# Splitting the maxima's rows and multiplying the gates on GpSimd instead of VectorE, in a two-branch attention kernel

## The chip, the core and the metric

The kernel runs on one core of a Trainium2 chip. The core has five engines with a queue of instructions each, executed in order: TensorE (PE, its weight loads shown as PEld), VectorE (DVE), ScalarE (ACT), GpSimd (POOL) and SyncE (SP), which here only issues DMAs. An engine waits at an instruction until the semaphores of the work it needs have come. The metric is the device time of one execution in microseconds (us); lower is better.

## The reference

Two attention blocks over the same input are mixed by a gate per token. There are 2048 tokens of 512 features and 32 heads of 16.

```python
x = A_x
g = sigmoid((x * gate_w).sum(-1, keepdims=True))
# A: causal softmax inside 4 segments of 512 tokens, plus a memory of earlier segments
logits = einsum("bhqd,bhkd->bhqk", qs, ks) * scale + mask
a_dot  = softmax(logits) @ vs
a_mem  = (phi(qs) @ M) / (phi(qs) @ z + 1e-6)     # M, z summed over earlier segments
a = (sigmoid(beta) * a_mem + (1 - sigmoid(beta)) * a_dot) @ wo_A
# B: full softmax attention over 2048 tokens
b = (softmax(q @ k.T * scale) @ v) @ wo_B
out = g * a + (1 - g) * b
```

## The kernel before

A unit is four heads (a group `qd` of 8) and 512 queries (a segment `c`). Units 0 to 31 are A, units 32 to 63 are B. After a stage of projections (up to about 370 us) the main loop runs 32 rounds, k = 0 to 31. In round k TensorE computes the transposed scores of unit 32+k in 32 groups (`t_group`, L528), then those of unit k in 5 groups; ScalarE takes their exponentials (L534), GpSimd masks the diagonal pieces of A (L537), and TensorE multiplies with the values (`pv`, L550).

The softmax needs each query's maximum before the exponential. It is found one round ahead: TensorE also computes the scores of the next units the other way round (`s_b` L474, `s_a` L452) into two banks `sbk`, and VectorE reduces each bank to maxima (L476, L460, L462). `m_chain(k+1)` then turns the maxima of a pair of units (tile `mx`, 128 queries x 32) into two fp32 rows: `hi`, the negated maximum rounded to the matmul's format, and the rest, both in the tile `m8` (named `m` in the profile). `m_rows(k+1)` transposes `m8` on TensorE (L501), ScalarE copies it out (L503, tile `mr`), and SyncE's DMAs (L509) write it as extra rows of the query tiles `qa` and `qb`, so that the score product subtracts the maximum by itself.

A unit is finished by `fin_copy` (L557 and a DMA to `pd`), `fin_load` (loads the output `o` and the softmax sums `rec`), `fin_rec` (L574 to L580: the reciprocal of the sums, times the gate `grow`, and for A times `nq` from beta, then a DMA to `rd`), `fin_bc` (L586: `rd` broadcast into `d`) and `fin_norm` (L590 on GpSimd: `o` times `d`). `load_wo` (L601 to L603) loads a piece of the two output weights and splits it on GpSimd into `wh` and `wl`; it runs in rounds 1 to 4.

The order is written out by hand. A round has iterations `it`, two groups of TensorE each, and the function `beside` puts the smaller work at an iteration: `fin_rec` of the B unit at 5, its `fin_bc` and the `fin_rec` of the A unit at 6, `fin_norm` of B at 9 and of A at 13 (every other round), the loads of the next A queries, keys and values at 6, `load_wo` at 9, `m_chain` at 10. `m_rows` follows in TensorE's order behind group 24, the first of iteration 12. Each engine's own queue has its pieces in the order of this code:

```python
            beside(k, it)
            if it == S_LAST:
                m_chain(k + 1)
```

with `S_LAST = 10`, and further down in the same loop body, still ahead of the next iteration,

```python
            if it == 9:
                if k % 2 == 0 and k < 30:
                    load_vb(k // 2 + 1)
                if 1 <= k <= 4:
                    load_wo(k - 1)
```

Of the kernel before, what the change touches and what calls it, by code (L numbers as in the profile page):

```python
# [12 lines left out]
OP = mybir.AluOpType  # L13
# [21 lines left out]
def gated_mix_kernel(ctx, tc, xt, wq, wk, wv, wo, beta, wqkv, wob, gate_w, out):  # L35
    nc = tc.nc
# [18 lines left out]
    grow = P.tile([128, 2, NC4, E], FT, name="grow")  # L55
    gh = P.tile([128, 4], FT, name="gh")
    nh = P.tile([128, 4], FT, name="nh")
    nq = P.tile([128, 8], FT, name="nq")
# [374 lines left out]
    def pair_max(k):  # L433
        if k not in MX:
            MX[k] = W.tile([128, 2, 4, 4], FT, name="mx")
        return MX[k]
# [43 lines left out]
    def m_chain(k):  # L480
        mx = pair_max(k)
        if k == 1:
            nc.vector.memset(mx[:, 0], 0.0)
        if k < 32:
            nc.vector.tensor_reduce(mx[:, 1], MXB.pop(32 + k).rearrange("q j p i c -> q (j p) i c"), axis=AX.X,
                                    op=OP.max)
        else:
            nc.vector.memset(mx[:, 1], 0.0)
        del MX[k]
        mx = mx.rearrange("q u h i -> q (u h i)")  # L490
        m8 = M8[k] = W.tile([128, 2, 32], FT, name="m8")
        hi = W.tile([128, 32], FR, name="mhi")
        nc.vector.tensor_scalar(hi, mx, -1.0, None, op0=OP.mult)
        nc.vector.tensor_copy(m8[:, 0], hi)
        nc.vector.scalar_tensor_tensor(m8[:, 1], mx, -1.0, hi, op0=OP.mult, op1=OP.subtract)

    def m_rows(k):
        m8 = M8.pop(k)
# [72 lines left out]
    def fin_rec(u):  # L571
        kd, qd, c = UN[u]
        r = AT.pop(("r", u))
        nc.vector.reciprocal(r, r)  # L574
        if kd == "A":
            nc.vector.scalar_tensor_tensor(r, r, nq[:, qd:qd + 1], grow[:, 0, c], op0=OP.mult, op1=OP.mult)
        else:
            nc.vector.tensor_tensor(r, r, grow[:, 1, c], op=OP.mult)
        AT["rd", u] = D.tile([128, E], FT, name=f"rd{u}")
        nc.sync.dma_start(AT["rd", u], r)  # L580

# [168 lines left out]
    for blk in range(16):  # L750
        g, c = divmod(blk, 4)
# [37 lines left out]
        if blk == 14:  # L789
            m_chain(0)  # L790
# [96 lines left out]
    def beside(k, it):  # L887

        for f, it0, u in ((fin_load, NT + 1, 32 + k), (fin_rec, 5, 31 + k), (fin_bc, 6, 31 + k),
                          (fin_load, 1, k - 1), (fin_rec, 6, k - 1), (fin_bc, S_LAST + 2, k - 1)):  # L890
            if it == it0 and (k or it0 > NT):
                f(u)
        c, j = divmod(k - 1, 8)
        if k and j % 2:
            for kd, it0 in (("B", 9), ("A", 13)):
                if it == it0:
                    fin_norm(kd, j // 2, c)
        if k >= 8 and k % 2 == 0 and it == NT + 2:
            out_split(k // 8 - 1, k // 2 % 4)
        if (k, it) == (31, 4):  # L900
            grest = AT["grest"] = AT["o"][0][64:, 0, 0]
            nc.sync.dma_start(grest, GD[3 * C:].rearrange("(o t) -> o t", o=1).to_broadcast([64, C]))
        if (k, it) == (31, 9):
            grest = AT["grest"]
            nc.vector.tensor_scalar(grest, grest, nh[64:, 3:4], None, op0=OP.mult)
        if (k, it) == (31, NT + 2):
            fin_rec(63)
        if k == 31 and it == 13:
            o = AT["o"][1][:64, 3, 0]
            nc.gpsimd.tensor_tensor(o, o, AT["d"][0][:64], op=OP.mult)  # L910
        if k == 31 and it < 8 and it % 2 == 0:
            for a in range(2):
                tail_split(it // 2, slice(0, 3), a)
# [18 lines left out]
    for k in range(32):  # L932
        ua, ub = k, 32 + k
        banks = T3 + [b[:, 0] for b in SBK] * (k == 31)
        for n in range(NG):
# [10 lines left out]
            if it == S_LAST:  # L946
                m_chain(k + 1)
# [74 lines left out]
```

## Time and profile before

| what | us |
|---|---|
| median of 3 runs | 1957.94 |
| lowest and highest | 1955.35, 1962.38 |
| the profiled execution | 1956.4 |
| its span | 1954.7 |
| VectorE busy, of the span | 1629.9 |
| GpSimd busy, of the span | 275.8 |
| one round of the main loop, before and after round 8 | 47.7, about 50.2 |

A row of the profile has the line of the kernel, the engine, the operation, out<-in by the names of the tiles, and the shapes. In a list in order of time the first number is the start in us from the start of the span, the second the length in us; the brackets at the end hold the idle time before and what ended it. In a list of waits the numbers are the total in us, how often, and the longest. In the chain, shares are of the span. The mean granted clock of TensorE over the execution was 0.999 of full speed.

### The profile page before, as it was taken

The page shows a single profiled execution, that of the slowest core. Times are in us where ns is not written, and L with a number is a line of the kernel's source. Part 1 is how long each engine was busy: PE and PEld are TensorE (multiplying, and loading weights), DVE is VectorE, ACT ScalarE, POOL GpSimd, SP SyncE. Part 2 cuts the span into 40 slices and gives each one's busy share as a digit, 9 for nine tenths or more (in the row PEclk, how much of TensorE's full clock was granted, in tenths as well). Part 3 has the DMA queues.
Part 4 walks back from the last instruction along what each step waited for, and adds up shares of the span by engine and source line. Part 5 has one row for each costly group of instructions (what it writes and reads, how often), then busy time and mean ns, then how long its engine had stood idle before and what let it go on. Part 6 is the DMA issues. An engine that isn't in the chain of part 4 may idle for free.

```text
span 1954.7 us, 43539 instructions
## 1 busy us (share of the span) xinstructions
PE 1930.3 (99%) x17485; PEld 939.3 (48%) x17485; DVE 1629.9 (83%) x1798; ACT 1433.4 (73%) x2699; POOL 275.8 (14%) x497
## 2 busy tenths in 40 slices
PE   7999999999999999999999999999999999999999
PEld 5887777444344444444444444444444444444445
DVE  7135766899999999999999999999999999999942
ACT  4233333688888888888888888888888888888884
POOL 5201000012120101111111111111111111111022
PEclk9999999999999999999999999999999999999999
DMA  7666655644444444343435453444354444434111
GB/s 218 170 205 188 198 192 178 156 98 115 98 115 93 106 91 109 81 111 80 114 87 115 87 115 87 113 87 115 87 115 87 109 86 96 101 88 106 48 50 58
DMA packets 163790, 222.49 MB, mean 114 GB/s; under 512 B 39916, under 2 KB 90556, under 8 KB 157828
## 3 DMA queue, kind: packets, MB, share of 16 engines
q1 hardware_dynamic: 159284, 211.41, 43.7%
q0 software_dynamic: 3248, 8.03, 2.1%
q8 instruction: 138, 2.26, 0.5%
q14 instruction: 64, 0.52, 0.1%
q10 hardware_dynamic: 1056, 0.26, 0.1%
HBM read 147.95 MB, written 68.16 MB: 111 GB/s over the span
## 4 chain that ended last, share of the span: by engine, by line
PE 95%; DVE 3%; ACT 1%; SPq 1%; DMA 1%; issue 0%; DVEq 0%; ACTq 0%
PE pvb L550 33%; PE tb L528 17%; PE sbk L474 12%; PE mb L528 9%; PE tb L304 4%; PE sbk L452 3%; PE tb L616 2%; PE mb L304 2%; PE sbk L287 1%; DVE mxb L476 1%; PE tb L287 1%; PE pvb L304 1%; PE mb L616 1%; PE sbk L456 1%; PE mb L287 1%; PE pvb L287 1%
## 5 line engine op out<-in xcount | busy, mean ns | idle before, releaser
L476 DVE TENSOR_REDUCE mxb<-sbk 128x2 f32<-128x1024 f32 x1024 | 1222.3, 1222 | 67.3 <-PE sbk L474 63.1
L534 ACT ACTIVATE raw<-tb 128x512 f32<-128x512 f32 x1555 | 887.5, 598 | 152.9 <-PE tb L528 89.6
L550 PE MATMUL pvb<-raw,vb 128*17 128x256 f32 (+1 forms) x8072 | 639.3, 388 | 0.0
L534 ACT ACTIVATE raw<-mb 128x512 f32<-128x512 f32 x782 | 467.6, 598 | 79.5 <-PE tb L528 44.8
L528 PE MATMUL tb<-qb,xh 64*128 64x512 f32 x872 | 331.6, 495 | 1.7 <-ACT raw L534 1.7
L550 PEld LDWEIGHTS pvb<-raw,vb 128*17 128x17 f32 x8072 | 134.4, 95 | 340.1 <-issue 336.6
L474 PE MATMUL sbk<-xh,qb 64*128 64x512 f32 x1344 | 281.5, 395 | 2.7 <-DVE mxb L476 1.8
L528 PE MATMUL mb<-qb,xh 64*128 64x512 f32 x445 | 220.6, 496 | 0.0
L537 POOL TENSOR_SCALAR_AFFINE_SELECT raw<-raw 128x256 f32<-128x256 f32 (+1 forms) x320 | 115.5, 361 | 709.6 <-ACT raw L534 701.7
L528 PEld LDWEIGHTS tb<-qb,xh 64*128 64x128 f32 x872 | 124.7, 183 | 179.6 <-issue 89.9
L528 PE MATMUL tb<-qb,kb 64*128 64x512 f32 x470 | 179.5, 496 | 1.3 <-DVE st L314 0.8
L460 DVE TENSOR_REDUCE mx<-sbk 128x2 f32<-128x768 f32 (+1 forms) x128 | 136.7, 1090 | 22.9 <-PE sbk L456 18.3
L474 PE MATMUL sbk<-kb,qb 64*128 64x512 f32 x704 | 146.4, 398 | 0.0
L474 PEld LDWEIGHTS sbk<-xh,qb 64*128 64x128 f32 x1344 | 138.3, 186 | 7.4 <-DVE mxb L476 5.0
L528 PEld LDWEIGHTS mb<-qb,xh 64*128 64x128 f32 x445 | 81.3, 183 | 95.2 <-issue 50.4
L590 POOL TENSOR_TENSOR o<-o,d 128x512 f32<-128x512 f32 x31 | 39.7, 1281 | 545.6 <-DMA d<-rd 461.9
L528 PEld LDWEIGHTS tb<-qb,kb 64*128 64x128 f32 x470 | 68.2, 183 | 100.1 <-issue 52.6
L528 PE MATMUL mb<-qb,kb 64*128 64x512 f32 x234 | 116.1, 496 | 0.0
L550 PE MATMUL pvb<-raw,va 128*17 128x256 f32 (+2 forms) x1280 | 94.7, 384 | 0.8 <-ACT pvs L559 0.8
L452 PE MATMUL sbk<-ka,qa 64*128 64x256 f32 (+3 forms) x512 | 88.2, 358 | 1.1
L528 PE MATMUL tb<-qa,ka 64*128 64x512 f32 (+3 forms) x339 | 79.5, 372 | 0.0
L311 ACT ACTIVATE st<-tb 128x512 fp32r<-128x512 f32 x33 | 19.8, 599 | 80.2 <-DVE phi L310 40.5
(284 smaller groups left out, 1837.6 us busy)
## 6 DMA issues: line engine op xcount, KB each, us to landing
xh<-dB SPq DMA_DIRECT2D x38, 512.0 KB
vb<-vdB SPq DMA_DIRECT2D x16, 1088.0 KB
dB<-st SPq DMA_DIRECT2D x64, 256.0 KB
dA<-st SPq DMA_DIRECT2D x64, 256.0 KB
pd<-pvs SPq DMA_DIRECT2D x64, 256.0 KB
kb<-dB SPq DMA_DIRECT2D x22, 512.0 KB
xh<-dB SPq DMA_DIRECT2D x38, 256.0 KB
qb<-dB SPq DMA_DIRECT2D x64, 128.0 KB
```

Source lines behind the costliest of these rows:

```text
L287: nc.tensor.matmul(b, lhs, WV[wi][:, k, :], start=n == 0, stop=n == 11)
L304: nc.tensor.matmul(b, WS[ws][w][wi][:, k, :], (XH, XL)[xi][c][:, k, :], start=n == 0, stop=n == 11)
L452: nc.tensor.matmul(b[:, j, c0:c0 + n], q_of(u)[r, p, i * 128:(i + 1) * 128], k_of(u, p)[r, :n], start=True, stop=False)
L460: nc.vector.tensor_reduce(m[:, :, p, i], b[:, :, :n], axis=AX.X, op=OP.max)
L474: nc.tensor.matmul(b[:, j], q_of(u)[r, p, i * 128:(i + 1) * 128], k_of(u, p)[r, kc * C:(kc + 1) * C], start=True, stop=True)
L476: nc.vector.tensor_reduce(MXB[u][:, :, p, i, kc], b, axis=AX.X, op=OP.max)
L528: nc.tensor.matmul(bs[j][:, c0:c0 + w], k_of(u, h // 2)[r, 128 * it:128 * it + 128], q_of(u)[r, h // 2, q0:], start=True, stop=True)
L534: nc.scalar.activation(pt, bs[j], AF.Exp, scale=SCALE)
L537: nc.gpsimd.affine_select(out=m, in_=m, pattern=[[1, 128]] if n < 2 else [[0, 2], [1, 128]], compare_op=OP.is_ge, fill=0.0, base=0, channe ...
L550: nc.tensor.matmul(PVB[32 * h:32 * h + E + 1, q0 + lo:q0 + hi], vt[:, it, 4 * q + h, :], pt[:, lo:hi], start=it == 0 and lo == 0, stop=it ...
L590: nc.gpsimd.tensor_tensor(o, o, d, op=OP.mult)
L616: nc.tensor.matmul(b, (AT["oh"], AT["ol"])[oi][:, g, a], (AT["wh"], AT["wl"])[wi][:, g, a], start=n == 0, stop=n == 11)
```

## The change

Two pieces of small arithmetic go from VectorE's queue to GpSimd's.

In `m_chain` the reduction of the maxima (L485) stays on VectorE. Negation, rounding, copy and rest are done on GpSimd, now with the negated maximum written back into `mx` by an operation of its own, so that three operations become four. The two memsets, each executed once in the kernel, move too. In `fin_rec` the reciprocal stays on VectorE; the multiplication with the gate moves, and for A the one instruction that multiplied by two factors becomes two.

```diff
     def m_chain(k):
         mx = pair_max(k)
         if k == 1:
-            nc.vector.memset(mx[:, 0], 0.0)
+            nc.gpsimd.memset(mx[:, 0], 0.0)
...
         else:
-            nc.vector.memset(mx[:, 1], 0.0)
+            nc.gpsimd.memset(mx[:, 1], 0.0)
...
-        nc.vector.tensor_scalar(hi, mx, -1.0, None, op0=OP.mult)
-        nc.vector.tensor_copy(m8[:, 0], hi)
-        nc.vector.scalar_tensor_tensor(m8[:, 1], mx, -1.0, hi, op0=OP.mult, op1=OP.subtract)
+        nc.gpsimd.tensor_scalar(mx, mx, -1.0, None, op0=OP.mult)
+        nc.gpsimd.tensor_copy(hi, mx)
+        nc.gpsimd.tensor_copy(m8[:, 0], hi)
+        nc.gpsimd.tensor_tensor(m8[:, 1], mx, hi, op=OP.subtract)
...
         nc.vector.reciprocal(r, r)
         if kd == "A":
-            nc.vector.scalar_tensor_tensor(r, r, nq[:, qd:qd + 1], grow[:, 0, c], op0=OP.mult, op1=OP.mult)
+            nc.gpsimd.tensor_scalar(r, r, nq[:, qd:qd + 1], None, op0=OP.mult)
+            nc.gpsimd.tensor_tensor(r, r, grow[:, 0, c], op=OP.mult)
         else:
-            nc.vector.tensor_tensor(r, r, grow[:, 1, c], op=OP.mult)
+            nc.gpsimd.tensor_tensor(r, r, grow[:, 1, c], op=OP.mult)
```

GpSimd's queue in round 1, from the masks of round 0 to those of round 1, before (`wh` and `wl` are the split output weights, `raw` the exponentials that are masked):

```order
L537 AFFINE_SELECT raw_86<-raw_86 128x2x128 x6
L602 CAST wh<-o_2775 128x512
L603 TENSOR_TENSOR wl<-o_2775,wh 128x512
L602 CAST wh<-o_2775 128x512
L603 TENSOR_TENSOR wl<-o_2775,wh 128x512
L537 AFFINE_SELECT raw_86<-raw_86 128x128 x4
```

The same place now (`rec` are the reciprocals of `fin_rec`, `m` the rows that L501 transposes; the lines below the changed ones have moved by up to two):

```order
L538 AFFINE_SELECT raw_86<-raw_86 128x2x128 x6
L580 TENSOR_TENSOR rec<-rec,grow 128x16
L577 TENSOR_SCALAR rec<-rec,nq 128x16
L578 TENSOR_TENSOR rec<-rec,grow 128x16
L604 CAST wh<-o_2776 128x512
L605 TENSOR_TENSOR wl<-o_2776,wh 128x512
L604 CAST wh<-o_2776 128x512
L605 TENSOR_TENSOR wl<-o_2776,wh 128x512
L493 TENSOR_SCALAR mx<-mx 128x32
L494 CAST mhi<-mx 128x32
L495 CAST m_3479<-mhi 128x32
L496 TENSOR_TENSOR m_3479<-mx,mhi 128x32
```

The gates' multiplications came in ahead of the output weights, the four operations on the maxima behind them.

VectorE's queue around the same `m_chain`, before:

```order
L476 TENSOR_REDUCE mxb<-sbk_115 128x2
L485 TENSOR_REDUCE mx<-mxb 128x16
L493 TENSOR_SCALAR mhi<-mx 128x32
L494 CAST m_3476<-mhi 128x32
L495 SCALAR_TENSOR_TENSOR m_3476<-mx,mhi 128x32
L476 TENSOR_REDUCE mxb<-sbk_114 128x2
```

And now:

```order
L476 TENSOR_REDUCE mxb<-sbk_114 128x2
L476 TENSOR_REDUCE mxb<-sbk_115 128x2
L485 TENSOR_REDUCE mx<-mxb 128x16
L476 TENSOR_REDUCE mxb<-sbk_114 128x2
L476 TENSOR_REDUCE mxb<-sbk_115 128x2
```

The three operations between the reduction L485 and the next reduction of scores are gone; the order on TensorE, ScalarE and SyncE is the same as before.

## The prediction

> **What bounds the kernel now.** I read the page's busy line and chain first, then one long window of the main loop, then the waits, and last the instructions in order of time around the two places that the change touches.
>
> ```profile
> PE 1930.3 (99%) x17485; PEld 939.3 (48%) x17485; DVE 1629.9 (83%) x1798; ACT 1433.4 (73%) x2699; POOL 275.8 (14%) x497
> PE 95%; DVE 3%; ACT 1%; SPq 1%; DMA 1%; issue 0%; DVEq 0%; ACTq 0%
> 1000.00:1500.00 500.00, 499.66 (x5026) 212.93 (x5020) 462.84 (x474) 412.70 (x768) 67.28 (x120) 1.00 0.44 99
> ```
>
> The third line is the window 1000 to 1500 us; after the length it gives PE, PEld, DVE, ACT, POOL, then the granted clock. TensorE is busy 499.66 of 500 us, VectorE 462.84. Busy matmuls can hide a wait, so the waits between 420 and 1880 us (the rounds k = 1 to 30 of the main loop) decide who is late:
>
> ```profile
> PE tb L528 <- ACT raw L534: 2.0, 7, 0.3
> PE sbk L474 <- DVE mxb L476: 0.7, 1, 0.7
> DVE mxb L476 <- PE sbk L474: 55.5, 70, 2.1
> ```
>
> In 1460 us TensorE waited once, 0.7 us, for VectorE, while VectorE waited 55.5 us for TensorE. So TensorE sets the pace, and VectorE, though 93% busy, is not what it waits for.
>
> **What leaves VectorE.** Lengths are min/median/max in ns, from the views of the tiles mx, m and grow:
>
> ```profile
> L493 DVE TENSOR_SCALAR mhi<-mx x33: 180/181/182, 311.7 to 1895.8; 128x32 fp32r<-128x32 f32 x33
> L494 DVE COPY m<-mhi x33: 180/181/183, 311.9 to 1896.0; 128x32 f32<-128x32 f32 x33
> L495 DVE SCALAR_TENSOR_TENSOR m<-mx,mhi x33: 183/186/1284, 312.0 to 1896.1; 128x32 f32<-128x32 f32 x33
> L578 DVE TENSOR_TENSOR rec<-rec,grow x32: 174/174/176, 414.1 to 1930.3; 128x16 f32<-128x16 f32 x32
> L576 DVE SCALAR_TENSOR_TENSOR rec<-rec,nq,grow x31: 233/235/236, 416.7 to 1893.1; 128x16 f32<-128x16 f32 x31
> ```
>
> 33 x (181 + 181 + 186) + 32 x 174 + 31 x 235 ns = 18.1 + 5.6 + 7.3 = 31 us, about 1 us a round. By the waits above this hides behind TensorE and is worth nothing on the path, except for the one L495 that took 1284 ns, met below. The two memsets happen once each; off VectorE or on GpSimd they cost nothing measurable.
>
> **What comes onto GpSimd.** Each m_chain becomes a multiplication, two copies and a subtraction of 128x32, each waiting for the one before. No such size ran there; the nearest rows are the 128x128 mask and the 128x128 addition, and for the gap between two dependent operations the wo pieces:
>
> ```profile
> 1326.77 0.29 POOL L537 TENSOR_SCALAR_AFFINE_SELECT raw<-raw 128x128 f32<-128x128 f32 x1 [40.31 <-ACT raw L534]
> L989 POOL TENSOR_TENSOR o<-o,d x4: 458/460/464, 1940.6 to 1945.6; 128x128 f32<-128x128 f32 x4
> 427.38 0.61 POOL L602 CAST wh<-o 128x512 fp32r<-128x512 f32 x1 [28.62 <-DMA o<-in_A_wo_dram]
> 428.08 1.28 POOL L603 TENSOR_TENSOR wl<-o,wh 128x512 fp32r<-128x512 f32 x1
> ```
>
> Between 128 and 512 elements the two-input operation grows by (1.28 - 0.46) / 384 = 2.1 ns an element, which leaves 0.19 us for none and gives 0.25 us for 32; the one-input ones I take at 0.17 us, below the 0.29 of the 128-wide mask. From the end of L602 (427.99) to L603 are 0.09 us. The chain: 3 x 0.17 + 0.25 + 2 x 0.09 = 0.95 us, plus 0.15 us to hand over, 1.1 us. Bounds: no cheaper than on VectorE, 4 x 0.18 = 0.7 us; no dearer than four of the 0.46 us addition with three gaps, 2.1 us. I take 1.1, since a shape of 32 lies far below 128.
>
> **Quiet rounds (28 of 32).** Who waits for m_chain is the transposing product L501, two groups later:
>
> ```profile
> 1313.55 0.21 DVE L485 TENSOR_REDUCE mx<-mxb 128x16 f32<-128x64 f32 x1
> 1314.10 0.18 DVE L495 SCALAR_TENSOR_TENSOR m<-mx,mhi 128x32 f32<-128x32 f32 x1
> 1316.45 0.39 PE L501 MATMUL tb<-ident,m 128*32 128x128 f32 x4
> ```
>
> L485 ends at 1313.76. On GpSimd the rows are ready at 1314.9, and 1316.45 is 1.6 us later: hidden, and even the dear bound (1315.9) is. What stands ahead in GpSimd's queue in an even round is fin_norm of B, which ends about 4 us before the chain:
>
> ```profile
> 1358.31 1.28 POOL L590 TENSOR_TENSOR o<-o,d 128x512 f32<-128x512 f32 x1 [24.55 <-DMA d<-rd]
> 1364.18 0.18 DVE L495 SCALAR_TENSOR_TENSOR m<-mx,mhi 128x32 f32<-128x32 f32 x1
> ```
>
> **Rounds 1 to 4.** There load_wo stands at it 9 and m_chain at it 10, so GpSimd, in order, has L602, L603, L602, L603 ahead of the chain, and the first of them waits for a DMA. These are the first and the last of the four, and L501, in each of the rounds:
>
> ```profile
> 430.00 1.28 POOL L603 TENSOR_TENSOR wl<-o,wh 128x512 fp32r<-128x512 f32 x1
> 429.15 0.39 PE L501 MATMUL tb<-ident,m 128*32 128x128 f32 x4
> 477.44 0.61 POOL L602 CAST wh<-o 128x512 fp32r<-128x512 f32 x1 [7.24 <-DMA o<-in_A_wo_dram]
> 480.05 1.28 POOL L603 TENSOR_TENSOR wl<-o,wh 128x512 fp32r<-128x512 f32 x1
> 476.85 0.39 PE L501 MATMUL tb<-ident,m 128*32 128x128 f32 x4
> 522.23 1.28 DVE L495 SCALAR_TENSOR_TENSOR m<-mx,mhi 128x32 f32<-128x32 f32 x1
> 524.10 1.27 POOL L603 TENSOR_TENSOR wl<-o,wh 128x512 fp32r<-128x512 f32 x1
> 525.57 0.39 PE L501 MATMUL tb<-ident,m 128*32 128x128 f32 x4
> 573.12 0.61 POOL L602 CAST wh<-o 128x512 fp32r<-128x512 f32 x1 [8.85 <-DMA o<-in_A_wo_dram]
> 575.72 1.29 POOL L603 TENSOR_TENSOR wl<-o,wh 128x512 fp32r<-128x512 f32 x1
> 573.05 0.39 PE L501 MATMUL tb<-ident,m 128*32 128x128 f32 x4
> ```
>
> GpSimd is free of the wo pieces at 431.28, 481.33, 525.37 and 577.01, and L501 stood at 429.15, 476.85, 525.57 and 573.05. In rounds 2 and 4 the pieces do not even begin before L501's old time. Everything behind L501 on TensorE waits with it.
>
> One thing shifts the wo loads themselves. They stand on SyncE's queue behind rd<-rec, which waits for fin_rec's product:
>
> ```profile
> 512.11 0.23 DVE L576 SCALAR_TENSOR_TENSOR rec<-rec,nq,grow 128x16 f32<-128x16 f32 x1
> 512.38 0.33 SPq L580 DMA_DIRECT2D rd<-rec  x1
> ```
>
> The product ends at 512.34 and the DMA is issued at once. For A, GpSimd does two operations of 128x16 (0.17 + 0.09 + 0.22 us and a hand-over of 0.1) in place of 0.23 us: 0.3 us later in rounds 1, 3 and 4. In round 2 I count nothing, since there rd<-rec of A stands behind the issue of d<-rd of B. So L501 can start at:
> - round 1: 431.28 + 0.3 + 1.1 = 432.7, 3.5 us late
> - round 2: 481.33 + 1.1 = 482.4, 5.6 us late
> - round 3: 525.37 + 0.3 + 1.1 = 526.8, 1.2 us late. Here 1.0 us had been lost already (525.57 - 476.85 is 48.72 us against 47.70 for the round before), because L495 took 1.28 us beside L603; that gain is in the 1.2
> - round 4: 577.01 + 0.3 + 1.1 = 578.4, 5.4 us late
>
> Together 15.7 us. TensorE has no slack to win it back.
>
> **The clock after a standstill.** The trace has one stretch in which TensorE had hardly any work, the one-column products of the gate, and then half the clock:
>
> ```profile
> 48.84 1.84 PE L203 MATMUL tb<-one,phi 128*128 128x1 f32 x16
> 52.33 2.92 PE L287 MATMUL tb<-wv,xh 128*128 128x512 f32 x8
> 56.75 2.05 PE L287 MATMUL mb<-wv,xh 128*128 128x512 f32 x8
> 59.56 2.02 PE L287 MATMUL pvb<-wv,xh 128*128 128x512 f32 x8
> 54.00:56.00 2.00, 2.00 (x6) 1.54 (x6) 0.00 (x0) 0.00 (x0) 0.61 (x2) 0.50 0.96 193
> ```
>
> 3.5 us (48.84 to 52.33) of it brought a granted clock of 0.50 in the window 54 to 56, and the 12 products that followed took 4.42 us (52.33 to 56.75) where the next 12 took 2.81: 1.6 us lost. Three of the stalls are as long as that stretch or longer. I count the price for the two longest, since 3.5 us is the very length seen, and get 3.2 us; the ends are none and three, 0 and 4.8 us.
>
> The Trainium skill, "TensorE: Matmul & The Clock Gate", section "What's actually happening", has the clock halve after an idle window of about 3.4 us that runs freely, and return after a busy one. By that rule a stall of 5.6 or 5.4 us holds a whole window about six times in ten and one of 3.5 us hardly ever, which as an estimate gives one fall, not two, and 17.3 us in all instead of 18.9. The trace agrees with the half rate and with a length of some 3.3 us (twice the 1.6 us lost); here the near-idle 3.5 us were enough.
>
> **The end.** fin_rec of the last block is some 0.15 us later. TensorE runs the output products from 1928.25 on without a gap, so this is hidden:
>
> ```profile
> 1928.25 8.57 PE tb L643 x36
> ```
>
> **Sum.** 15.7 + 3.2 = 18.9 us on the profiled execution's 1956.4 us (span 1954.7 and 1.7 around it): 1975.3. The median of the runs, 1957.94, lies 1.5 us above that execution; I say 1976.
>
> **Rivals.**
> - Only the stalls, no fall of the clock: 1972 to 1974. For it: the window in which the clock is judged may lie badly. Against: the stretch at 48.84.
> - GpSimd's chain is dearer than any row, because small operations cost far more there than their size. It decides from 2.7 us on (1313.76 to 1316.45); at 4 us a chain, 28 quiet rounds lose 1.3 us each, 36 us, and the four others 2.9 us each, 12 us more: about 2024. Against: the bound of 2.1 us.
> - Faster: TensorE's modelled ends hide a real wait for VectorE. Place: the reuse of the two sbk banks behind L476. 1 us a round would be 31 us less against 15.7 us of stalls: about 1942. It decides from 0.5 us a round. Against: VectorE waits for TensorE, not the other way.
> - The wo pieces land early enough not to matter, and nothing moves: 1957. It would take DMAs 4 to 6 us quicker in three rounds.
>
> **How the numbers follow.** The forecast with a fall of the clock has 0.62, without one 0.20, the dear chain 0.08, faster 0.05, no move 0.05. With the chain at 0.7 and no fall the sum is 15.7 - 1.6 = 14.1 us, at 2.1 with three falls 15.7 + 4.0 + 4.8 = 24.5 us: 1970 to 1982, on either basis. 0.3% of the time, 5.9 us, is about what a measurement can tell here: slower 0.90, same 0.05, faster 0.05.
>
> **What would show it.** L501's group has TensorE waiting for GpSimd in rounds 1 to 4 only, some 3.5, 5.6, 2.2 and 5.4 us; the copies and subtraction of m_chain stand right behind the second wl piece there; the clock row drops to 0.5 once to three times between 430 and 590 us; the rounds from 5 on keep their 47.7 to 50.3 us; VectorE's busy time falls by 31 us. I am wrong if later rounds grow (dear chain), shrink (VectorE was the bound), or if the wo pieces end before L501 is due.

## The result, and the profile after

The changed kernel takes 1980.88 us (median of 4 runs, 1980.01 to 1982.61) against 1959.2 us before: 1.0113 times as long, with a 95% interval of 1.0092 to 1.0133. The forecast was 1976 us with a range of 1970 to 1982. The execution that was profiled took 1982.61 us, its span is 1980.9 us, 26.2 us more than the span before.

First the page of the kernel after, its busy line and its chain:

```profile
PE 1939.8 (98%) x17485; PEld 942.4 (48%) x17485; DVE 1617.6 (82%) x1634; ACT 1433.6 (72%) x2699; POOL 332.0 (17%) x725
PE 90%; DMA 3%; DVE 3%; issue 2%; POOL 1%; SPq 1%; ACT 1%; DVEq 0%; ACTq 0%; POOLq 0%
```

TensorE's share of the chain fell from 95% to 90%; DMA rose from 1% to 3%, issue from 0 to 2%, and GpSimd came in with 1%. The waits of TensorE between 400 and 1900 us, of which before none came to more than 2.3 us in total, name the place:

```profile
PE tb L502 <- POOL m L495: 14.1, 4, 6.4
PE tb L529 <- ACT raw L535: 2.3, 8, 0.3
```

Four waits, 14.1 us, at L502 (L501 before), for L495, the copy into `m8` that now runs on GpSimd. In order of time, GpSimd in round 2 and TensorE's product that waits for it:

```profile
489.13 0.61 POOL L604 CAST wh<-o 128x512 fp32r<-128x512 f32 x1 [7.11 <-DMA o<-in_A_wo_dram]
489.82 1.26 POOL L605 TENSOR_TENSOR wl<-o,wh 128x512 fp32r<-128x512 f32 x1
491.02 0.61 POOL L604 CAST wh<-o 128x512 fp32r<-128x512 f32 x1
491.71 1.26 POOL L605 TENSOR_TENSOR wl<-o,wh 128x512 fp32r<-128x512 f32 x1
492.94 0.29 POOL L493 TENSOR_SCALAR mx<-mx 128x32 f32<-128x32 f32 x1
493.29 0.21 POOL L494 CAST mhi<-mx 128x32 fp32r<-128x32 f32 x1
493.57 0.21 POOL L495 COPY m<-mhi 128x32 f32<-128x32 f32 x1
493.74 0.25 POOL L496 TENSOR_TENSOR m<-mx,mhi 128x32 f32<-128x32 f32 x1
```

The four operations of `m_chain` stand right behind the second `wl`, which had to wait for the weights' DMA. The product in rounds 0 to 5 (its start in us, and in brackets the wait ahead of it):

```profile
389.33 0.39 PE L502 MATMUL tb<-ident,m 128*32 128x128 f32 x4
439.52 0.62 PE L502 MATMUL tb<-ident,m 128*32 128x128 f32 x4 [2.19 <-POOL m L495]
493.83 0.85 PE L502 MATMUL tb<-ident,m 128*32 128x128 f32 x4 [6.44 <-POOL m L495]
545.03 0.62 PE L502 MATMUL tb<-ident,m 128*32 128x128 f32 x4 [1.03 <-POOL m L495]
597.40 0.85 PE L502 MATMUL tb<-ident,m 128*32 128x128 f32 x4 [4.47 <-POOL m L495]
646.90 0.39 PE L502 MATMUL tb<-ident,m 128*32 128x128 f32 x4
```

From round 0 to round 5 it is 257.57 us; before it was 620.75 - 381.44 = 239.3. That is 18.2 us of the loss. Of the rest, none lies behind round 5: from its product to that of round 30 it takes 1246.8 us in both kernels (1246.76 after, 1246.83 before). 7.9 us lie ahead of round 0, whose product stood at 381.44 before and at 389.33 now; the last experiment section comes back to it. Behind the wait of round 2 the clock fell, in the window 490 to 500 us (the columns are those of the windows shown before: length, five engines, clock, DMA share, GB/s):

```profile
490.00:500.00 10.00, 6.17 (x36) 2.30 (x40) 2.55 (x3) 2.72 (x6) 3.79 (x7) 0.53 0.05 15
```

### The profile page after: what moved, and what is told of

Read it like the earlier page. It is cut to its first block, busy times and chain, and to the rows that moved or that the text cites. A ratio compares the mean times of both kernels' runs of the same rounds, so it can differ in the third digit from the quotient of the medians.

```text
span 1980.9 us, 43700 instructions
## 1 busy us (share of the span) xinstructions
PE 1939.8 (98%) x17485; PEld 942.4 (48%) x17485; DVE 1617.6 (82%) x1634; ACT 1433.6 (72%) x2699; POOL 332.0 (17%) x725
## 4 chain that ended last, share of the span: by engine, by line
PE 90%; DMA 3%; DVE 3%; issue 2%; POOL 1%; SPq 1%; ACT 1%; DVEq 0%; ACTq 0%; POOLq 0%
PE pvb L551 31%; PE tb L529 16%; PE sbk L474 11%; PE mb L529 8%; PE tb L304 4%; PE sbk L452 3%; PE tb L618 2%; PE mb L304 2%; PE sbk L287 1%; PE tb L287 1%; PE mb L618 1%; PE pvb L304 1%; DVE mxb L476 1%; DMA o<-in_A_wo_dram 1%; PE sbk L456 1%
## 5 line engine op out<-in xcount | busy, mean ns | idle before, releaser
L476 DVE TENSOR_REDUCE mxb<-sbk 128x2 f32<-128x1024 f32 x1024 | 1239.5, 1221 | 103.6 <-PE sbk L474 100.0
L580 POOL TENSOR_TENSOR rec<-rec,grow 128x16 f32<-128x16 f32 x32 | 7.1, 222 | 491.2 <-DVE rec L575 491.2
```

The lines of the kernel that those rows point to most:

```text
L476: nc.vector.tensor_reduce(MXB[u][:, :, p, i, kc], b, axis=AX.X, op=OP.max)
```

## The experiments

The measure used throughout is the time from the transposing product (L501 or L502) of round 0 to that of round 5, in the profiled execution: the four rounds with `load_wo` lie in it, and nothing that happens earlier or later. The whole times are medians, each against runs of the kernel before on the same chip.

| kernel | round 0 to 5, us | waits of TensorE for GpSimd there | whole, us | ratio, 95% interval |
|---|---|---|---|---|
| before | 239.3 | none | 1959.2 | 1 |
| after | 257.6 | 2.19, 6.44, 1.03, 4.47 | 1980.88 | 1.0113 (1.0092 to 1.0133) |
| only m_chain moved | 261.8 | 2.48, 5.40, 3.03, 3.62 | 1982.81 | 1.0117 (1.0098 to 1.0135) |
| only the gates moved | 239.6 | none | 1958.15 | 0.9988 (0.9977 to 1.0) |
| after, load_wo behind m_chain | 238.6 | none | 1958.99 | 1.0 (0.9988 to 1.0012) |
| before, load_wo behind m_chain | 238.6 | none | 1958.87 | 0.9997 (0.9987 to 1.0007) |
| after, waits overfilled | 271.3 | two filled, 3.75 and 2.18 left | 1992.24 | 1.0172 (1.0155 to 1.019) |
| after, waits filled | 253.3 | filled, 2.3 left in all | 1972.13 | 1.0062 (1.0042 to 1.0083) |
| load_wo behind, chain + 5 copies | 238.7 | none | 1958.77 (one run) | |
| load_wo behind, chain + 12 copies | 246.5 | 1.4 to 1.6 in every round | 2010.7 (one run) | |

### Which half of the change costs

The first kernel has only the change of `m_chain`, the second only that of `fin_rec` (the hunks are those of the change).

> Only m_chain goes to GpSimd, fin_rec stays on VectorE. Measure: from the transposing product of round 0 to that of round 5, which took 239.4 us before and 257.6 after. Theory (m_chain stands behind the wo pieces in GpSimd's queue): nearly all of the loss is here, 256 to 257.6 us; the whole some 0.9% over before. Rival (the gates' products, through SyncE's queue or the VectorE-GpSimd port, cost a good part): under 252 us.

> Only fin_rec's products go to GpSimd, m_chain stays on VectorE. Theory: 239.4 us from round 0 to round 5 (within 0.6), the whole like before within 0.2%. Rival (the gates cost): 243 us or more.

With `m_chain` alone the whole loss is there, 261.8 us, even 4 us more than forecast: its waits of 14.5 us are like those of the full change, but three of the four are now longer than 3 us, and the clock fell behind all four, behind the one of 2.48 us too, where with the full change it fell behind two. TensorE's wait of round 1 and the windows behind rounds 1 and 3:

```profile
434.65 0.86 PE L502 MATMUL tb<-ident,m 128*32 128x128 f32 x4 [2.48 <-POOL m L495]
430.00:440.00 10.00, 7.52 (x64) 2.62 (x60) 5.45 (x6) 4.96 (x11) 4.52 (x8) 0.83 0.03 7
540.00:550.00 10.00, 8.28 (x56) 3.04 (x56) 4.59 (x4) 4.62 (x9) 1.75 (x5) 0.66 0.06 18
```

The gates alone cost nothing: 239.6 us, and 1958.15 us in the whole. The rival that they delay something through SyncE's queue falls.

### The place in the queue

Nothing of the arithmetic is changed here; `load_wo` is called behind `m_chain` instead of ahead of it, once in the kernel after and once in the kernel before:

```diff
             if it == S_LAST:
                 m_chain(k + 1)
+            if it == S_LAST and 1 <= k <= 4:
+                load_wo(k - 1)
...
             if it == 9:
                 if k % 2 == 0 and k < 30:
                     load_vb(k // 2 + 1)
-                if 1 <= k <= 4:
-                    load_wo(k - 1)
```

> The whole change, but load_wo is called behind m_chain (iteration 10 in place of 9). Theory (queue order alone): no wait of TensorE for GpSimd at the transposing product, 238.5 us from round 0 to round 5 (five rounds of 47.7), clock 1.00 throughout, the whole like before or 1 us under it; VectorE's 31 us are worth nothing. Rival (GpSimd's slower chain or the shared port costs in every round): rounds above 47.7 and 50.2 us, the whole over before by 6 us or more. Rival (relief of VectorE is worth something once the stall is gone): the whole under before by 6 us or more.

> The kernel before, with load_wo behind m_chain as the only edit. Theory: the 1.0 us that before lost in round 3, where a VectorE operation with two SBUF inputs lasted 1.28 us beside GpSimd's subtraction, is gone: 238.5 us from round 0 to round 5, the whole like before. If it is 242 or more, moving load_wo has a price of its own, and the kernel with both edits has to be read against this one.

With the move the changed kernel has no wait for GpSimd and no loss: 238.6 us. Round 2 of it, GpSimd's last two operations of the chain, the first of the wo pieces, and TensorE's product:

```profile
477.30 0.21 POOL L495 COPY m<-mhi 128x32 f32<-128x32 f32 x1
477.47 0.25 POOL L496 TENSOR_TENSOR m<-mx,mhi 128x32 f32<-128x32 f32 x1
480.04 0.61 POOL L604 CAST wh<-o 128x512 fp32r<-128x512 f32 x1 [2.31 <-DMA o<-in_A_wo_dram]
479.25 0.39 PE L502 MATMUL tb<-ident,m 128*32 128x128 f32 x4
```

The row that L495 copies into `m8` is ready 1.7 us ahead of its product, the second row 1.5 us, and the late DMA holds up only the pieces themselves. The same move in the kernel before gives the same 238.6 us, so it has no price of its own, and its gain of 0.7 us is that of round 3, where VectorE no longer ran L495 for 1.28 us. It was not quite as forecast: in round 3 the pieces still began beside the chain, and L494 took 0.51 us instead. (With the gates alone moved, L495 lasted 1.28 us again in round 3, and the round 48.98 us.)

The two kernels with the move differ in nothing but the change under study, and stand at 1958.99 and 1958.87 us. So the relief of VectorE is worth nothing on the path, and GpSimd's use costs nothing in the quiet rounds. TensorE's busy time in the window 1000 to 1500 us says the same: 499.66 before, 499.66 after, and 499.67 in the changed kernel with the move.

### How much the chain may cost

Five and twelve copies of `mx` onto itself lengthen the chain on GpSimd, on top of the kernel with `load_wo` behind `m_chain`:

```diff
         nc.gpsimd.tensor_scalar(mx, mx, -1.0, None, op0=OP.mult)
+        for _ in range(12):
+            nc.gpsimd.tensor_copy(mx, mx)
         nc.gpsimd.tensor_copy(hi, mx)
```

> As the kernel with load_wo behind m_chain, and five further copies of mx onto itself in m_chain on GpSimd: the chain is longer by 1.1 to 1.4 us. Theory (the chain has 1.6 us to spare in every round): nothing changes, 238.5 us from round 0 to round 5, later pairs of rounds 100.3 us. Rival (no spare time): 1.1 us or more a round.

> The same with twelve further copies, 2.5 to 3.4 us. Theory: the transposing product waits 0.9 to 1.8 us in each of the 32 rounds, the whole 29 to 56 us over before, without a fall of the clock since each wait is short. Rival (other work covers it): within 10 us of before.

Five copies took 1.3 us and cost nothing (238.7 us). Twelve made the span 52 to 53 us longer (2009.0 us against 1957.0 with five and 1956.0 with none); some 5 us of it lie ahead of round 0, the rest is that of the waits. GpSimd ran ten of the copies in 2.65 us, and TensorE waited in each of the rounds 0 to 29:

```profile
485.86 2.65 POOL L495 COPY mx<-mx 128x32 f32<-128x32 f32 x10
PE tb L504 <- POOL m L497: 31.9, 23, 1.6
PE mb L504 <- POOL m L497: 9.6, 7, 1.4
```

Twelve copies are 3.2 us, of which 1.7 were spare: 1.4 to 1.6 us of wait and 0.23 us more for the second half of the product, which waits for the subtraction. This is the rival of the dear chain, brought about by an edit: its point of decision is where the quiet round had put it. Thirty waits of this size brought no fall of the clock.

### The clock behind the waits

To see what the standstill itself costs, TensorE is given products of the identity with itself ahead of the transposing product, so that it stands still less while it waits. Their result is overwritten and enters nothing.

```diff
-        b = misc()[0:64, :128]
+        bb = misc()
+        for n in range({2: 8, 3: 21, 4: 4, 5: 15}.get(k, 0)):
+            nc.tensor.matmul(bb[:, :128], ident, ident, start=True, stop=True)
+        b = bb[0:64, :128]
```

The first version had 60 products in round 2 and 44 in round 4 (`{3: 60, 5: 44}`).

> The kernel after, with 60 and 44 products of the identity with itself (128x128, results overwritten) put on TensorE ahead of the transposing product in rounds 2 and 4, some 5.3 and 3.9 us, a little less than its waits there (6.4 and 4.5 us). Theory (the standstill halves the clock): the waits end at the same time, but the granted clock stays 1.00 behind them; from round 0 to round 5 253.5 us in place of 257.6. Rival (the time lost behind the waits has another cause, such as late DMAs or ScalarE): 257 us or more with the same slow stretch.

It missed: each product became two matmuls of 0.11 us, and the 60 took 13.66 us instead of 5.3, so that the whole was 11 us slower than the change. It still answered for the clock: from the product of round 2 at 501.21 to that of round 3 it took 49.85 us, which is a plain round of 47.7 and the wait of 2.18 in round 3. The second version, with the counts of the diff, was set by this price.

> As the kernel with filling products, with fewer of them: 8, 21, 4 and 15 in rounds 1 to 4. One of them takes 13.66 us / 60 = 0.23 us as measured there, so these are 1.8, 4.8, 0.9 and 3.4 us, each below the wait it fills. Theory (the standstill halves the clock): granted clock 1.00 throughout, and the time from round 0 to round 5 is five rounds of 47.7 us, the waits' 14 to 15.5 us with the filling counted in, and up to 1 us around the products: 253 to 255 us, in place of 257.6 (after) and 261.8 (m_chain alone on GpSimd). Rival (the time behind the waits has another cause): 257 us or more.

253.3 us, with the granted clock 1.00 behind every wait. The windows that held 0.53 and 0.75 after the change:

```profile
490.00:500.00 10.00, 9.86 (x95) 4.79 (x93) 6.42 (x6) 6.28 (x13) 2.57 (x7) 1.00 0.05 18
590.00:600.00 10.00, 8.93 (x82) 4.98 (x80) 4.76 (x5) 4.65 (x10) 3.89 (x7) 1.00 0.06 17
```

Work that does nothing but keep TensorE going wins back 4.2 us of the 18.2. The waits with their fillings come to 14.8 us over five rounds of 47.7, much like the 15.0 us of the change (14.1 us of waits and 0.23 us more for each product, which comes in two halves), so the gain is the clock's and not that of shorter waits. The median of the whole gains 8.7 us (1972.13 against 1980.88). In part that is the choice of the execution: the profiled one with filled waits was the slowest of its four (1977.99 us; the others took 1969.55 to 1973.74), and lost clock ahead of round 0 as well (0.66 in the window 320 to 330). The rest is not explained by these traces.

### The 7.9 us ahead of round 0

In the profile after, TensorE waited 4.5 us for keys that were still on their way, ahead of the product of round 0 (before 0.5 us, by the same view):

```profile
PE sbk L474 <- DMA xh<-dB: 4.5, 1, 4.5
```

The first changed operation runs at 314.5 us, and the stage was 2.7 us late by 312 already. The 4.0 us by which the wait for the keys was longer come on top, and behind this wait the clock fell as well, which cost about 1 us more:

```profile
320.00:330.00 10.00, 6.25 (x23) 4.40 (x24) 4.96 (x6) 0.07 (x1) 0.45 (x1) 0.66 0.62 171
```

These three make up 7.7 of the 7.9 us. In the ten profiles the product of round 0 stands between 381.4 and 389.3 us (with the wait of 1.6 us taken off where the chain has twelve copies more): 383.7 with the change and `load_wo` behind, 384.7 without the change and with the move, 385.3 with the gates alone, 388.3 with the filled waits. Kernels with and without the change lie mixed; the kernel before was the earliest of all and the one after the latest. I take it for the spread of a stage that waits for DMAs, since code that is equal up to there has 381.4 and 384.7 without the change, and 383.7, 386.5, 388.3 and 389.3 with it; that this alone makes up the 3.5 us by which the medians differ beyond 18.2 was not shown.

## Why the prediction was right, and where it was off

- **What bounds the kernel.** Right. TensorE sets the pace; 31 us of arithmetic taken off VectorE changed none of the rounds 5 to 30. The forecast that VectorE's busy time falls by 31 us was wrong: it fell by 12.3 (1629.9 to 1617.6). The groups of the main reduction, before and after, show why:

```profile
L476 DVE TENSOR_REDUCE mxb<-sbk 128x2 f32<-128x1024 f32 x1024 | 1222.3, 1222 | 67.3 <-PE sbk L474 63.1
```

```profile
L476 DVE TENSOR_REDUCE mxb<-sbk 128x2 f32<-128x1024 f32 x1024 | 1239.5, 1221 | 103.6 <-PE sbk L474 100.0
```

  The mean of one is the same, the busy time of the group is 17 us more. The 1024 lengths add up to 1251 us, so 29 us of them overlapped before and 11 us now: reductions that follow each other without a pause overlap at their ends, and with VectorE less behind, fewer of them did.
- **The chain's price.** 1.1 us was forecast, from L485's end at 644.22 in round 5 to the end of the subtraction at 645.36 it is 1.14. Errors cancelled in part: the single operations are 0.29, 0.21, 0.21 and 0.25 us where I had 0.17 three times and 0.25, while the handing over took less and the last two overlap, since the subtraction needs the rounded maxima of L494 and not the copy before it; that each operation waits for the one before was wrong. The gate's two products for A take 0.33 and 0.22 us, where I had 0.17 and 0.22.
- **Quiet rounds.** Right: 1.6 us to spare were forecast, and twelve copies of 3.2 us made a wait of 1.4 to 1.6.
- **Rounds 1 to 4.** Right in place and cause, shown by the move of one call. The waits were forecast as 3.5, 5.6, 2.2 and 5.4 us, 16.7 in all, and were 2.19, 6.44, 1.03 and 4.47, 14.1 in all. They end 0.86 us behind the last `wl` piece in all four rounds, not 1.1, because the product's first half needs only the copy L495; its second half, behind the subtraction, then costs 0.23 us more, 15.0 us in all. The term that was off is the landing of the wo loads with the 0.3 us counted for the gates, read from one execution. In round 2 the first piece began 0.6 us after L501's start before (477.44 against 476.85), and 1.7 us after its due time now (489.13 against 439.52 + 47.7 + 0.2); in the other rounds and kernels it moves by some 0.3 to 2 us, earlier or later.
- **The clock.** Two falls were forecast, 1.6 us each, and two came, behind rounds 2 and 4. From product to product, with the waits and the second halves taken off, the fall behind round 2 cost 2.2 us and the one behind round 4 cost 1.6. The filled waits show that the standstill is the cause. That it was two falls is in part luck: with `m_chain` alone four came, behind waits of 2.48 to 5.40 us, and the last section shows what a fall depends on, which the forecast did not have. The falls are no accident of one execution: the mean clock is 0.992 or 0.993 in all four of the change, and 0.997 to 1.000 in 25 of the kernel before. As a sum, 18.9 us was forecast for the rounds and 18.2 came; stalls that were too long and falls that were too cheap made up for each other.
- **The size of the whole.** 1976 was forecast (its own sum on the median is 1957.94 + 18.9 = 1976.8) and 1980.88 came, inside the range. As a loss that is 21.7 us against 1959.2, of which 18.2 are the rounds that the forecast was about. No step of the forecast has the other 3.5, nor the 7.9 us ahead of round 0 in the profiled execution.
- **The rivals.** The dear chain, the gain from VectorE and the early wo pieces each fell by a run or a trace of their own. Stalls without a fall of the clock, and one fall with 17.3 us, fell by the trace of the change, which has two.

## What to carry to other kernels

Before work is moved to an engine that stands idle, look not at its busy share but at what stands ahead of the new place in its queue, and at what that waits for: GpSimd was 14% busy, and the four rounds in which a DMA wait came ahead of a row that TensorE needed cost the whole 1%. The remedy is the order of two calls and not the engine. Relief of an engine that itself waits for the bound is worth nothing, however busy it is: the waits between the two tell which of them is late.

## What the runs showed of the hardware

- TensorE's clock halves behind waits shorter than I had counted on. It fell behind a wait of 2.48 us (m_chain alone, round 1), behind one of 2.18 us (overfilled, round 3: 0.83 in the window 550 to 560) and behind one of 1.93 us for keys (gates alone, 317 us), not behind one of 2.19 us (after, round 1), and behind none of the thirty of 1.4 to 1.6 us. The Trainium skill, "TensorE: Matmul & The Clock Gate", section "What's actually happening", gives about 3.4 us of a freely running window; a fall that sometimes follows and sometimes not fits a free window, but the measured waits are shorter than it. The traces suggest what decides, though no run was made to test it. In them every spell of half clock lasts 3.4, 6.8 or 10.2 us, but for the last, which the end of the execution cuts off, and in each trace the spells begin whole multiples of 3.41 us apart. On this grid, here three windows of the kernel after around its wait of 2.19 us, then two of the overfilled one around its wait of 2.18 (the first figure behind the length is TensorE's busy time, the last but two the clock):

```profile
434.58:438.00 3.42, 2.75 (x32) 0.88 (x24) 3.41 (x3) 2.76 (x6) 3.06 (x4) 1.00 0.03 10
438.00:441.41 3.41, 1.89 (x18) 0.82 (x20) 0.60 (x2) 1.07 (x3) 1.56 (x5) 1.00 0.00 0
441.41:444.82 3.41, 3.41 (x36) 1.19 (x36) 3.40 (x4) 3.01 (x7) 0.00 (x0) 1.00 0.08 25
548.38:551.80 3.42, 1.24 (x14) 0.47 (x9) 1.22 (x1) 0.89 (x3) 2.63 (x6) 1.00 0.00 0
551.80:555.21 3.41, 3.41 (x24) 0.98 (x22) 1.56 (x2) 2.05 (x5) 0.00 (x0) 0.50 0.06 14
```

  The grid cut the wait of 2.19 us into 0.67 and 1.52, and left the one of 2.18 whole. From 300 us to the end of the main loop, in all ten traces, the clock fell behind each of the 15 windows at full clock in which TensorE stood still for 1.81 us or more, and behind none with 1.53 us or less. So a window need not be idle as a whole: about half of it was enough, and a wait of 1.9 us can be one too long where one of 2.2 us is not.
- Useless products of 1.2 to 5.0 us on TensorE, put into its waits, kept the clock at 1.00 and made the kernel faster than without them (1972.13 against 1980.88 us).
- Operations of 128x32 on GpSimd take 0.29 us (product with a constant), 0.21 (copy) and 0.25 (subtraction of two tiles), and copies that depend on each other follow every 0.27 us.
